# Which early tile takes its second layer direct, and where batch 1's Fourier units stand, in a kernel of spectral mixing and a two-layer network

## The chip, the cores and the metric

The kernel runs on one core of a Trainium2 chip. TensorE (PE) multiplies matrices into PSUM, VectorE (DVE) and ScalarE (ACT) read PSUM and write SBUF, GpSimd (POOL) works on SBUF alone, and SyncE (SP) only issues transfers; GpSimd's queue issues transfers too. Each engine takes its instructions in the order of the program. The metric is the device time of one execution in microseconds (us), as a median of several runs.

## The reference

The input x has 8 batches of 3008 rows and 256 channels. Each batch goes through a real Fourier transform along the rows, is multiplied by a filter of 1505 frequencies, and goes back; then all 24064 rows pass a network of 256, 2048 and 256 channels with an exact Gelu.

```python
X = np.fft.rfft(x, axis=1)
Y = X * (filt_r + 1j * filt_i)[None, :, :]
y = np.fft.irfft(Y, n=x.shape[1], axis=1)      # 8 x 3008 x 256
h = y.reshape(24064, 256) @ w_in               # 256 -> 2048
g = 0.5 * h * (1.0 + erf(h / np.sqrt(2.0)))
out = g @ w_out                                # 2048 -> 256
```

## The kernel before

**Tiles and slots.** The network works on 47 tiles of 512 rows. A tile has 16 slots; slot s of the program is slot s mod 16 of tile s // 16. In each slot `mm1` (L640) makes one sixteenth of the tile's first layer, two matmuls of 512 columns, and ScalarE turns it into g by a Gelu (L643). Between them stands a sixteenth of the second layer of the tile before. Everything else is put into the slots by hand, with a table `at` that maps slots to calls; calls of a slot are emitted ahead of its matmuls.

**Second layer.** Most tiles use `mm2_seven` (L714): seven products of half-size matrices in place of eight, 112 matmuls of 128 columns, 7 a slot. They need sums of quarters of g, which VectorE makes on SBUF in the tile's last slots and the next tile's first ones: `sums_1` (L685, four instructions), `sums_2` (L691, two) and `sums_3` (L696, two, into s4_sb), and small adds of PSUM results (L729 to L743). A tile in the list `plain` uses `mm2_first` (L656) in their place: 64 matmuls of 256 columns, 4 a slot, no sums, two copies (L660). Before the change `plain` is tiles 0 and 2. The last tile of batch 0, tile 5, has another pace (`late`): in its first six slots stands only the second layer of tile 4.

**Fourier work.** Batch 0 is transformed in the prologue, up to about 38 us. Batches 1 to 7 are transformed beside the network. For a batch: `load_x_pairs` (GpSimd's queue) brings x, `fold` (VectorE, L109, L110) adds and subtracts its halves, `s1` is stage 1 (L430), whose results go through DRAM (R1) and come back as b_sb with `r1` (SP's queue). Three units follow, each with `s2` (stage 2, L457), `s2_out` (four products with the filters Fu on VectorE, L468), `s2_sum` (four sums, L474 and L475), `s3` (stage 3, L488) and its evacuation `s3_out` into v_sb, from where it goes through DRAM (R2) and returns as d_sb with `r2`. `s4` (stage 4, L515) multiplies d_sb with the table T4a and writes the rows y that `mm1` reads. The slots of batch 1's units are `s2 = (30, 44, 58)`, with stage 3 eleven slots later; `r2` of its first quarter comes four slots behind the last stage 3, and the first `s4` stands at slot 82, which does not depend on these.

**Filters and tables.** The filters are loaded into F, and `move_filters` copies them from SBUF to SBUF into Fu on SP's queue, by quarters c = 0 to 3: 16 moves in the prologue for a unit's first pair, 20 at slot 18 for the other two units. When F is read out its memory is used anew: s4_sb, v_sb and T4a all lie in it. T4a is made by `table_4_all` on GpSimd in four parts of six instructions (L410, L412), before the change at slots 47, 54, 101 and 114, from the factors that `table_4_factors` makes at slot 38. Scratch tiles tmp_sb for it and the d_sb tiles share a pool of three buffers.

**Gates.** `gate` (L142) is a GpSimd copy of one element. It makes GpSimd's queue wait until that element has been written, and with it all that stands behind: `load_next` puts one ahead of each group of x loads. For the last groups of batch 2 it reads d_sb of batch 1. One gate at slot 101 reads the last a_sb of batch 2's stage 1.

**Output rows.** `put_rows` (L761) issues them, mostly on GpSimd's queue, for tiles 0 and 1 partly on SP's. The buffers (ost and t_sb) are four, used in turn.

**PSUM.** Three banks are of kind h (first layer, one of stage 2 and one of stage 3), two of kind o (second layer), three of kind f (the other banks of stages 1 to 3, and table factors).

Of the kernel before, what the change touches and what calls it, by code (L numbers as in the profile page):

```python
# [31 lines left out]
class _Mix:  # L32
# [87 lines left out]

    def move_filters(self, m0, m):

        for c in range(4):
            for q in range(2):
                for e in range(2):
                    o, k = 32 * c + 16 * q, 6 * c + m0
                    for t in ((0, 1),) if c or m0 == 0 else ((0,), (1,)):
                        t = slice(t[0], t[-1] + 1)
                        i = self.F[32 * q + e:32 * q + 32:2, t, k:k + m, :]
                        self.nc.sync.dma_start(  # L130
                            out=self.Fu[o:o + 16, t, e ^ q, m0:m0 + m, :].rearrange("p t m c -> p t (m c)"),
                            in_=i.rearrange("p t m c -> p t (m c)"))
# [281 lines left out]
    def s1(self, b, c):  # L414

        nc = self.nc
        if c == 0:
            self.st[b, "R1"] = self.dram.tile([NB, 48, 256], BF16, tag="R1", name="R1")
        if b == 1 and c == 3:
            at = self.pp.tile([128, 2, 4, 256], BF16, tag="p12", name="p12").rearrange("p t k c -> p (t k) c")  # L420
        else:
            at = self.pa.tile([128, 8, 256], BF16, tag="a", name="a_sb")
        self.st[b, "a"] = at
        x = self.st[b, "s", c], self.st["x1"][:, 1, 4 * c:4 * c + 4]
        lent = "o" if b == 1 and c < 2 else "h"
        ps = [[self.bank("ps_s1", lent if i == v == 0 else "f") for v in range(2)] for i in range(2)]
        for i in range(2):
            for d in range(2):
                for v in range(2):
                    nc.tensor.matmul(ps[i][v][64 * d:64 * d + 64, :], lhsT=self.T1s[64 * v:64 * v + NA],  # L430
                                     rhs=x[d][64 * v:64 * v + NA, 2 * i:2 * i + 2, :], start=True, stop=True)
        for i in range(2):
            for v in range(2):
                w = 4 * v + 2 * i
                self._evac(at[:, w:w + 2, :].rearrange("p w c -> p (w c)"), ps[i][v], "act" if v else False)
        for d in range(2):
            for v in range(2):
                w = HB * d + 16 * v + 4 * c
                nc.sync.dma_start(out=self.st[b, "R1"].rearrange("n q c -> q n c")[:, w:w + 4],
                                  in_=at[64 * d:64 * d + 48, 4 * v:4 * v + 4])  # L440
# [204 lines left out]
    def mm2_first(self, t, lo, hi):  # L645

        nc = self.nc
        for n in range(lo, hi):
            if t:
                q, jc = n // 16, n % 16  # L650
            else:
                jc, q = (n // 2, n % 2) if n < 32 else (n % 16, n // 16)
            if jc == 0 and (q % 2 == 0 if t else q < 2):
                self.st["o2", q // 2 if t else q] = self.bank("ps_o", "o").rearrange("p (a b) -> p a b", a=2)
            ps, a = (self.st["o2", q // 2], q % 2) if t else (self.st["o2", q % 2], q // 2)
            nc.tensor.matmul(ps[:, a, :], lhsT=self.st["g", t][:, jc, q * 128:q * 128 + 128],  # L656
                             rhs=self.w_out_sb[:, jc, :], start=(jc == 0), stop=(jc == 15))
            if jc == 15 and (q % 2 if t else q > 1):
                ost = self.po.tile([128, 2, 256], FP32, tag="ost", name="ost")
                nc.vector.tensor_copy(out=ost, in_=ps)  # L660
                for i in range(2):
                    self.put_rows(t * TCH + ((q - 1 + i) if t else (q - 2 + 2 * i)) * 128, ost[:, i],
                                  nc.gpsimd if t else nc.sync)

    def weight_sums(self):

# [116 lines left out]
def kernel(  # L783
# [9 lines left out]
    m = _Mix(ctx, tc, x, filt_r, filt_i, moe_w_in, moe_w_out, out)  # L793
    nc, B, S = tc.nc, m.B, m.S
# [3 lines left out]
    g = m.small  # L798
# [109 lines left out]
    at = {}  # L908

    def put(slot, f, *a):  # L910
        at.setdefault(slot, []).append((f, a))

    def first(b):
        return (b * S // TCH) * 16

    busy, crowd, after = set(), set(), {}
    for b in range(1, B):
        hi = first(b)
        e = 4 * (b == B - 1)
        s1, n1, r1 = (4, 3.3, 17) if b == 1 else (hi - 87, 3.7, hi - 73) if b == 2 else (hi - 94 - e, 3.7, hi - 80 - e)  # L920
        s2 = (30, 44, 58) if b == 1 else (hi - 74, hi - 59, hi - 44) if e else (hi - 64 + (b == 2), hi - 48, hi - 32)
        busy.update(range(s1 - 1, s1 + int(3 * n1) + 2))
        for c in range(4):
            slot = (4, 8, 11, 13)[c] if b == 1 else s1 + int(c * n1)
            put((0, 1, 5, 8)[c] if b == 1 else (70, 74, 86, 94)[c] if b == 2 else hi - 94 - (20, 13, 8, 6)[c], m.fold, b, c)
            put(slot, m.s1, b, c)
        for u in range(3):
            put(r1 if u < 2 else s2[0] + 1, m.r1, b, u)
            put(s2[u], m.s2, b, u)
            for i in range(4):  # L930
                put(s2[u] + 2 * i + (b == 2 and u == 0), m.s2_out, b, u, i // 2, i % 2)
            for i in range(2):
                put(s2[u] + (9 + i if 1 < b < B - 1 else 7 + 2 * i), m.s2_sum, b, 2 * u + i)
            s3 = s2[u] + (11 if b == 1 else 12 if e or (b, u) in ((2, 0), (B - 2, 2)) else 13)
            put(s3, m.s3, b, u)
            put(s3 + 1, m.s3_out, b, u, 1)
            busy.update(range(s2[u] - 1, s2[u] + 5), range(s3 - 1, s3 + 2))
        after[b] = s3 + 4
        crowd.update(range(s2[0], after[b]), range(s1 + 66, s1 + 94))
        if b + 1 < B:  # L940
            for i, (u, o, p) in enumerate(((0, 5, 1), (0, 7, 1), (1, 1, 2), (1, 5, 3), (1, 7, 3), (2, 1, 4), (2, 5, 5), (2, 7, 5))):
                put((76, 77, 80, 81)[i - 4] if b == 1 and i > 3 else s2[u] + o, m.load_next, b, p, i // 2, i % 2)
# [27 lines left out]
    put(9, m.table_u_pick, g)  # L970
    put(9, m.table_4_rows, g)
    put(9, m.weights_4, g)
    put(24, m.table_u)
    put(38, m.table_4_factors, g)
    put(101, lambda: m.gate(m.st[2, "a"][0:1, 3, 0:1]))
    parts = [(w, h) for w in range(0, HB, 8) for h in range(2)]
    for i, slot in enumerate((47, 54, 101, 114)):
        put(slot, m.table_4_all, parts[2 * i:2 * i + 2])
    put(18, m.move_filters, 2, 4)
    put(20, m.weight_sums)  # L980
    plain = (0, 2)
    seven = [t for t in range(NT) if t not in plain]
    for t in seven:
        for i, s in enumerate((12, 13, 15, 16 if t == S // TCH - 1 else 17)):
# [6 lines left out]
    for s in range((NT + 1) * 16):  # L991
        t, jc = s // 16, s % 16
# [44 lines left out]
```

## Time and profile before

| | |
|---|---|
| median of 3 runs | 738.75 us (738.12 to 739.8) |
| profiled execution | 738.78 us, its span 736.7 us |
| VectorE's products L468 | 84 x 1217 ns |
| VectorE's sums L685, L691, L696 | 180 x 690, 90 x 687, 90 x 697 ns |
| output rows on GpSimd's queue L761 | 231 x 575 ns |
| x loads on GpSimd's queue L101 | 156 x 516 ns |
| moves of filters at slot 18 | 20, issued from 55.94 to 69.9 us |
| first Gelu of tiles 1, 2, 3, 4, 6 | 52.87, 65.10, 81.39, 96.59, 130.50 us |

A row of a timeline has the start in us from the span's start, the duration in us, the engine, the line of the kernel, the operation, the tile written and those read with their shapes, and how many such instructions were put together (x2). In brackets stands for how long the engine had been idle before it, and on whom it waited. Matmul ends are modelled, so what is exact of a matmul is its start. Where several instructions are put together, their pitch is the distance to the next start divided by their number.

### The profile page before, as it was taken

To read this page: it belongs to the slowest core of one execution; us is meant where nothing else is said; L and a number is where in the kernel's file an instruction comes from. 1 tells how busy PE (TensorE), PEld (TensorE's weight loads), DVE (VectorE), ACT (ScalarE), POOL (GpSimd) and SP (SyncE) were. 2 spreads that over 40 slices of the span, in tenths; PEclk is the share of its full clock that TensorE was granted. 3 is DMA by queue.
4 is the path that set the end of the run, shared out by engine and by line. 5 is a ranking of instruction groups with operands and counts; after the bars stand their busy time and mean duration, and the time that the engine had idled before them with its cause. 6 is when DMAs were issued, how large, how long until landed. Compare 5 with 4: busy or idle time off the path is not lost.

```text
span 736.7 us, 22328 instructions
## 1 busy us (share of the span) xinstructions
PE 723.3 (98%) x9213; PEld 506.1 (69%) x9213; DVE 602.8 (82%) x1105; ACT 575.6 (78%) x1049; POOL 285.9 (39%) x545
## 2 busy tenths in 40 slices
PE   8999999999999999999999999999999999999998
PEld 4755665677777766676677767666677767777776
DVE  8886797899887998789986989779998898675566
ACT  6997766788887888778887788877888788777773
POOL 7943745686122653134521355114631131122121
PEclk9999999999999999999999999999999999999999
DMA  9885526655345553555545455455544433311011
GB/s 147 155 183 135 150 77 131 190 155 107 86 126 177 123 101 101 146 149 119 115 126 172 104 113 125 116 151 132 121 108 126 149 101 108 103 39 49 30 58 59
DMA packets 81254, 87.73 MB, mean 119 GB/s; under 512 B 13393, under 2 KB 61137, under 8 KB 81153
## 3 DMA queue, kind: packets, MB, share of 16 engines
q0 software_dynamic: 22288, 39.50, 24.1%
q1 hardware_dynamic: 58449, 46.62, 23.2%
q8 instruction: 72, 1.18, 0.7%
q10 hardware_dynamic: 416, 0.20, 0.1%
q14 instruction: 29, 0.24, 0.1%
HBM read 54.00 MB, written 46.66 MB: 137 GB/s over the span
## 4 chain that ended last, share of the span: by engine, by line
PE 87%; POOL 4%; DMA 3%; issue 3%; DVE 3%; ACT 1%; SPq 0%; DVEq 0%; POOLq 0%
PE ps_h L640 40%; PE ps_o L714 36%; PE ps_s L515 3%; PE ps_s L430 2%; PE ps_s L488 1%; DMA b_sb<-R 1%; PE ps_s L457 1%; POOL tmp_sb L410 1%; POOL out_dram L761 1%; DMA x_sb<-in_x_dram 1%; PE ps_c L587 1%; ACT y_sb L325 1%; POOL x_sb L101 1%; PE ps_o L656 1%; PE ps_c L565 0%
## 5 line engine op out<-in xcount | busy, mean ns | idle before, releaser
L643 ACT ACTIVATE g_sb<-ps_h 128x512 f16<-128x512 f32 x752 | 445.5, 602 | 137.2 <-PE ps_h L640 129.0
L640 PE MATMUL ps_h<-y_sb,w_in_sb 128*128 128x512 bf16 (+3 forms) x1600 | 445.4, 366 | 1.5 <-DVE a_sb L327 1.2
L761 POOL DMA_DIRECT2D out_dram<-ost x231 | 131.4, 575 | 373.9 <-DVE ost L743 365.5
L714 PEld LDWEIGHTS <-g_sb 128*128 128x128 f16 x2880 | 188.8, 98 | 83.4 <-issue 14.6
L640 PEld LDWEIGHTS <-w_in_sb 128*128 128x128 bf16 x1600 | 125.7, 98 | 9.3 <-issue 2.9
L714 PE MATMUL ps_o<-w_sums,g_sb 128*128 128x128 f16 x1440 | 124.8, 219 | 0.4 <-DVE g_sb L691 0.2
L714 PE MATMUL ps_o<-w_sums,s_sb 128*128 128x128 f16 x1440 | 123.3, 219 | 0.0
L714 PEld LDWEIGHTS <-s_sb 128*128 128x128 f16 x1440 | 97.0, 98 | 37.5 <-issue 2.1
L685 DVE TENSOR_TENSOR s_sb<-g_sb 128x1024 f16<-128x1024 f16 x180 | 118.6, 690 | 0.7 <-ACT g_sb L643 0.6
L714 PE MATMUL ps_o<-w_out_sb,g_sb 128*128 128x128 f16 x1440 | 116.4, 219 | 0.1
L468 DVE TENSOR_TENSOR p<-ps_s,Fu 128x1024 bf16<-128x1024 f32 x84 | 101.9, 1217 | 8.9 <-PE ps_s L457 7.3
L101 POOL DMA_DIRECT2D x_sb<-in_x_dram x156 | 79.5, 516 | 1.9 <-DMA x_sb<-in_x_dram 0.7
L691 DVE TENSOR_TENSOR g_sb<-s_sb,g_sb 128x1024 f16<-128x1024 f16 x90 | 61.7, 687 | 1.5
L696 DVE TENSOR_TENSOR F<-g_sb 128x1024 f16<-128x1024 f16 x90 | 62.8, 697 | 0.0
L714 PE MATMUL ps_o<-w_out_sb,F 128*128 128x128 f16 x720 | 62.5, 219 | 0.0
L714 PEld LDWEIGHTS <-F 128*128 128x128 f16 x720 | 48.3, 98 | 16.0 <-issue 0.8
L736 DVE TENSOR_TENSOR t_sb<-t_sb,ps_o 128x256 f32<-128x256 f32 x45 | 18.8, 417 | 41.9 <-PE ps_o L714 41.4
L515 PEld LDWEIGHTS <-d_sb 96*128 96x128 bf16 x448 | 31.3, 97 | 26.1 <-issue 1.3
L325 ACT ACTIVATE F<-ps_s 128x512 bf16<-128x512 f32 x83 | 45.5, 608 | 3.3 <-PE ps_s L488 3.2
L325 ACT ACTIVATE y_sb<-ps_s 128x376 bf16<-128x376 f32 x95 | 45.5, 479 | 3.2 <-PE ps_s L515 3.2
L743 DVE TENSOR_TENSOR ost<-t_sb,ps_o 128x256 f32<-128x256 f32 x88 | 32.9, 415 | 14.0 <-PE ps_o L714 14.0
L327 DVE CAST a_sb<-ps_s 128x512 bf16<-128x512 f32 x54 | 34.7, 684 | 11.3 <-PE ps_s L430 11.1
(159 smaller groups left out, 574.6 us busy)
## 6 DMA issues: line engine op xcount, KB each, us to landing
out_dram<-ost POOLq DMA_DIRECT2D x127, 128.0 KB, 2.9
b_sb<-R SPq DMA_DIRECT2D x21, 512.0 KB, 4.9
R<-F SPq DMA_DIRECT2D x84, 128.0 KB, 2.4
d_sb<-R SPq DMA_DIRECT2D x56, 192.0 KB, 3.8
R<-a_sb SPq DMA_DIRECT2D x108, 96.0 KB, 2.2
x_sb<-in_x_dram POOLq DMA_DIRECT2D x48, 94.0 KB, 2.6
x_sb<-in_x_dram POOLq DMA_DIRECT2D x48, 48.0 KB, 2.7
x_sb<-in_x_dram POOLq DMA_DIRECT2D x12, 188.0 KB, 5.1
```

The costliest lines, as they stand in the source:

```text
L101: self.nc.gpsimd.dma_start(out=xt[64 * v + to:64 * v + to + m, h, 4 * c:4 * c + 4 * n, :], in_=xv[h][at:at + m, w:w + 4 * n, :])
L325: self.nc.scalar.activation(out=out, in_=in_, func=AF.Copy, scale=1.0 if scale is None else scale)
L327: self.nc.vector.tensor_copy(out=out, in_=in_)
L468: v(out=w[:, a], in0=ps.unsqueeze(2).to_broadcast([128, 2, 2, 256]), in1=f.unsqueeze(1).to_broadcast([128, 2, 2, 256]), op=ALU.mult)
L515: nc.tensor.matmul(ps[:, 94 * i:94 * i + 94], lhsT=d[:, (grp % 2) * 4 + i, 128 * half:128 * half + 128], rhs=self.T4a[:, 4 * grp + i, 0:2 ...
L640: nc.tensor.matmul(ps[:, o:o + n], lhsT=w[:, dc], rhs=self.ring[:, dc, off:off + n], start=(dc == 0), stop=(dc == 1))
L643: nc.scalar.activation(out=self.st["g", t][:, jc, :], in_=ps, func=AF.Gelu)
L685: self.nc.vector.tensor_tensor(out=self.st["s", t][:, i:i + 2], in0=a, in1=b, op=ALU.subtract)
L691: self.nc.vector.tensor_tensor(out=a21[:, k], in0=self.st["s", t][:, k, 0], in1=a22[:, k], op=ALU.add)
L696: self.nc.vector.tensor_tensor(out=self.s4_sb[:, k], in0=a12[:, k], in1=s2[:, k], op=ALU.subtract)
L714: nc.tensor.matmul(ps[:, (m + 1) % 2, sub, :], lhsT=a[:, i, 128 * sub:128 * sub + 128], rhs=b[:, i], start=i == 0, stop=i == 7)
L761: eng.dma_start(out=out, in_=tile_[lo - r0:lo - r0 + n])
```

## The change

Tile 1 becomes the direct one, and tile 2 takes the seven products. Batch 1's stage 2 moves from slots 30, 44, 58 to 26, 39, 53, with stage 3 at 37, 51, 65 (before 41, 55, 69); with them `r2`'s first quarter (73 to 69) and the first four x loads of batch 2 (35, 37, 45, 49 to 31, 33, 40, 44). The four table parts move to slots 67, 82, 98 and 105, and ahead of the first three stands a gate on the last sum of tile 3, 4 or 5; the gate on a_sb goes. The table factors move from 38 to 48, `table_u` from 24 to 23. The quarters of `move_filters` are taken in reversed order. Since the two-copy form now has tile 1, its last row block goes to SP's queue, as in the seven-product form.

```diff
     def move_filters(self, m0, m):
-        for c in range(4):
+        for c in (3, 2, 1, 0):
...
             at = self.pa.tile([128, 8, 256], BF16, tag="a", name="a_sb")
-        self.st[b, "a"] = at
...
-                                  nc.gpsimd if t else nc.sync)
+                                  nc.gpsimd if t > 1 or t and q + i < 4 else nc.sync)
...
-        s2 = (30, 44, 58) if b == 1 else (hi - 74, hi - 59, hi - 44) if e else (hi - 64 + (b == 2), hi - 48, hi - 32)
+        s2 = (26, 39, 53) if b == 1 else (hi - 74, hi - 59, hi - 44) if e else (hi - 64 + (b == 2), hi - 48, hi - 32)
...
-            s3 = s2[u] + (11 if b == 1 else 12 if e or (b, u) in ((2, 0), (B - 2, 2)) else 13)
+            s3 = s2[u] + ((11, 12, 12)[u] if b == 1 else 12 if e or (b, u) in ((2, 0), (B - 2, 2)) else 13)
...
-    put(24, m.table_u)
-    put(38, m.table_4_factors, g)
-    put(101, lambda: m.gate(m.st[2, "a"][0:1, 3, 0:1]))
+    put(23, m.table_u)
+    put(48, m.table_4_factors, g)
+    for t, slot in ((3, 67), (4, 82), (5, 98)):
+        put(slot, lambda t=t: m.gate(m.st["s", t][0:1, 7, 1, 255:256]))
     parts = [(w, h) for w in range(0, HB, 8) for h in range(2)]
-    for i, slot in enumerate((47, 54, 101, 114)):
+    for i, slot in enumerate((67, 82, 98, 105)):
         put(slot, m.table_4_all, parts[2 * i:2 * i + 2])
...
-    plain = (0, 2)
+    plain = (0, 1)
```

## The prediction

> **What bounds the kernel now.** I read the page first, then the waits, then the timelines of the stretch from 55 to 135 us, engine by engine.
>
> ```profile
> PE 723.3 (98%) x9213; PEld 506.1 (69%) x9213; DVE 602.8 (82%) x1105; ACT 575.6 (78%) x1049; POOL 285.9 (39%) x545
> PEclk9999999999999999999999999999999999999999
> ```
>
> TensorE is busy for 98% of the span at a granted clock of 0.999, and the change takes no matmul away. So only time in which TensorE stands can be won. A late tile without any Fourier work takes 13.16 us (first Gelu of tiles 45 and 46: 701.29 and 714.45), which is 16 slots of 0.82. Tiles 2 to 5 took 65.40 us (first Gelu of tile 2 at 65.10, of tile 6 at 130.50). Their work, priced at pitches of undisturbed stretches: 4 x 13.16, plus 0.8 for the direct tile, 5 stage-2 and stage-3 blocks x 0.6, 4 stage-4 blocks x 0.166, 3 stage-1 blocks x 0.67 and 0.5 for the table factors = 59.6. So about 5.8 us are lost there, and from tile 6 on next to nothing. TensorE's timeline shows where:
>
> ```profile
> 71.99 0.42 PE L488 MATMUL ps_s<-p,U 32*64 32x256 bf16 x16
> 73.25 0.65 PE L488 MATMUL ps_s<-p,U 32*64 32x256 bf16 x16 [0.84 <-DVE p L474]
> ...
> 99.99 0.42 PE L488 MATMUL ps_s<-p,U 32*64 32x256 bf16 x16
> 101.94 0.65 PE L488 MATMUL ps_s<-p,U 32*64 32x256 bf16 x16 [1.52 <-DVE p L474]
> ...
> 121.49 0.28 PE L714 MATMUL ps_o<-w_out_sb,F 128*128 128x128 f16 x2
> 123.01 1.02 PE L640 MATMUL ps_h<-y_sb,w_in_sb 128*128 128x512 bf16 x4 [1.25 <-DVE a_sb L327]
> ```
>
> Stage 3 of units 0 and 2 of batch 1 stands between its halves, because VectorE's stage-2 sums (L474) are late: 73.25 against 72.28 and 101.94 against 100.27 (a half takes 0.28), 0.97 + 1.67 us. At 121.5 the next matmul is 1.41 late for an evacuation. With 0.37 at 113.9 that is 4.4 us in four places; the rest up to 5.8 is small change around them. I take 5.5 as what can be won, nearer to the sum over the tiles because that also has the small change; 4.4 and 5.8 are its ends.
>
> Why VectorE is late: in slots 28 to 41 it does tile 1's sums (L685, L691, L696) and unit 0's products together, and later GpSimd's table parts stretch it:
>
> ```profile
> 58.96 1.28 DVE L685 TENSOR_TENSOR s_sb<-g_sb 128x1024 f16<-128x1024 f16 x2
> ...
> 71.06 0.42 DVE L475 TENSOR_TENSOR p<-p 128x512 bf16<-128x512 bf16 x1
> ...
> 84.66 1.20 DVE L474 TENSOR_TENSOR p<-p 128x512 bf16<-128x512 bf16 x1
> ...
> 92.54 2.06 DVE L685 TENSOR_TENSOR s_sb<-g_sb 128x1024 f16<-128x1024 f16 x2
> ```
>
> (The same kinds take 0.42 and 1.28 undisturbed, 1.20 and 2.06 beside GpSimd's L410 and L412.)
>
> The stop at 121.5 is the end of another chain, read in GpSimd's and VectorE's rows:
>
> ```profile
> 112.23 0.18 POOL L142 COPY gate<-d_sb 1x1 bf16<-1x1 bf16 x1 [12.38 <-DMA d_sb<-R]
> 116.26 2.89 POOL L761 DMA_DIRECT2D out_dram<-ost  x5
> ```
>
> ```profile
> 119.67 0.42 DVE L737 TENSOR_TENSOR ost<-t_sb,ps_o 128x256 f32<-128x256 f32 x1 [1.71 <-DMA out_dram<-ost]
> 120.34 0.68 DVE L109 TENSOR_TENSOR x_sb<-x_sb 111x1024 bf16<-111x1024 bf16 x1
> ```
>
> GpSimd's queue stands 12.38 us at the gate for batch 1's first stage-4 tile; behind it are batch 2's x loads and tile 3's output rows; a buffer of these holds L737, and fold and evacuation stand behind L737.
>
> **The change part by part.**
>
> *Direct tile.* Tile 1's second layer (64 matmuls of 256 columns, a slot 0.87) runs beside tile 2, and tile 2's seven products beside tile 3. The 0.8 us moves a tile ahead: net 0. VectorE is relieved in slots 28 to 40 of 4 x 0.69 + 2 x 0.69 + 2 x 0.70 = 5.5 us of sums and has them in 44 to 56 instead; the seven small adds (0.42 each) go the same way and two copies (0.69 each) the other. This decides units 0 and 2 below.
>
> *Unit 0 at slot 26.* TensorE reaches it at 59.2; b_sb of unit 0 landed at 58.73 in the trace's record of its semaphore. Its four products (pitch 1.13) and four sums (pitch 0.34), with the copy of tile 0, end at about 66.2; stage 3 at slot 37 comes at 68.6. The 0.97 and its restart go. Stage 3's evacuation writes where the moved filters lie (v_sb is a part of F): with the reversed order quarter 1 is moves 9 to 12, issued by 64.8, quarter 2 moves 5 to 8; at the median of 2.6 both have landed by about 67.4, and the evacuation comes after 69.
>
> *Unit 1 at slot 39.* TensorE is there at 70.9, the first product at 71.6 if all 20 moves of the second filter set have landed. In the profile the last was issued at 69.32 and landed near 71.6. But batch 2's first x loads now start near 63, not 69.93, under these moves. Bounds: 0 and 2.5 us later (the worst landing of these moves, 5.1, against the median 2.6). VectorE's work until stage 3 at slot 51 (8 products and sums, two copies, tile 2's sums) ends near 81, TensorE is there at 83: 2 us of cover hide all but 0.5 of the upper end, so I take 0, ends 0 and 0.5.
>
> *Two slots between stage 3 and the next stage 2* (37 to 39, 51 to 53; before 41 to 44, 55 to 58). Stage 2 needs three banks of kind f that stage 3 fills. In the profile ScalarE frees them 2.0 and 2.6 us after stage 3's end at 73.9 (75.37 1.10 for the last two). Two slots and half a stage 2 are 2.0 us: 0.5 lost the first time, 0.2 the second, where VectorE takes one of the four. Ends 0 and 1.3. New cost 0.7.
>
> *Unit 2 at slot 53.* From the product at 85.6 VectorE has 4 products, 4 sums, two L696, two L685 and five small adds until stage 3 of slot 65: 4 x 1.13 + 4 x 0.34 + 4 x 0.61 + 1.9 = 10.2 us. TensorE needs 12 x 0.82 + 0.6 = 10.4. Before it was 11 slots with 1.3 us of stretching (0.8 + 0.56), and 1.67 were lost. I take 0.3 lost, ends 0 and 1.9.
>
> *Table parts.* Parts 1 and 2 (5.6 us each: 79.91 to 85.58; 6.2 under load, 90.13 to 96.34) leave slots 47 to 58, where they stretched VectorE by some 2.9 us (four L474 and L475 from 82.97 take 3.2 for 1.7, the pair at 92.54 0.8 more, an L685 at 95.65 0.56 more). Part 1 now waits for tile 3's last sum (slot 65), then runs from about 100.5 to 106.5 beside tile 4's folds and sums. VectorE's work in that tile is 13 instructions of 0.6 and 8 of 0.35, 10.6 of 13.2 us, so 2.6 are to spare; stretching seven instructions by 0.4 is 2.8. I take 0, ends 0 and 0.7. Three gates more on GpSimd: 0.2 each, in idle time. Behind the new gate in GpSimd's queue stand the x loads and tile 3's output rows.
>
> [...]
>
> *Gate and chain.* Stage 3 of unit 2 is four slots earlier. From its end (102.6) to the gate's release (112.23) is 9.6 us; from 96.7 this gives 106.3, about when table part 1 ends (106.5). Then 4.0 us to the rows (112.23 to 116.26) and 3.4 to L737's release (116.26 to 119.67): 114.1. TensorE's side of L737 was ready at 118.0; with 3.3 us won by then, 114.7. The 1.41 and the 0.37 go, with 0.6 us in hand; I keep 0.3, ends 0 and 1.4.
>
> *Third stage-4 transfer.* Its d_sb now lies in the buffer of table part 3, so the SP queue waits at slot 108 for it and stage 2's last load of batch 2 stands behind. Part 3 ends near 134.5 and slot 108 is near 136; the data is needed at slot 121, 10.7 us later, and such a transfer takes 3.8: covered by 6 us, 0. Without that cover each us of part 3's lateness would be one of TensorE's.
>
> *Moves in the prologue.* All 16 now wait for the last filter loads (quarter 3 first), so they start near 22 and not at 13.46, and end near 34; SP's next work is at 43.65: 0. GpSimd's copy at 18.90 waits for a filter load beside which they ran; ends -1.5 (VectorE's wait of 1.56 at 19.97 gone) and 0. I take -0.1, since these moves were some 5% of the DMA share there.
>
> *One row of tile 1 to SP, table_u and table factors moved:* behind VectorE's copy, 0.
>
> Sum: -5.5 + 0.7 + 0.3 + 0.3 - 0.1 = -4.3. The profiled execution took 738.78 us (span 736.7 and 2.1 around it), 0.03 from the median of 738.75: 734.45, so 734.5 us. All upper ends of the costs together (0.5 + 1.3 + 1.9 + 0.7 + 1.4, on 4.4 won) are +1.4, all lower ends -7.3.
>
> **Rivals.** *VectorE stays late (A).* It now has tile 2's sums and units 1 and 2 in 26 slots, saturated again; for it 10.2 against 10.4 us. Each 1 us there is 1 us for TensorE and for the chain behind. Loss 1.0 to 2.3: 735.5 to 736.8.
>
> *GpSimd becomes the bound (B).* Gate, part 1, x loads and rows make an unbroken chain of 0.2 + 6 + 4 + 3.4 us from tile 2's rows on. If it is 2 to 4 us late (VectorE's late sums, output issues of 0.59), L737 and the fold wait again: 736.8 to 738.5. Against it: it has 12.38 us less standing.
>
> *Slower (C).* Parts 3 and 4 run back to back in tile 6, from 128 to 140, where VectorE was busy 7.7 and 9.2 of 10 us and idle 3.1 of 20. Twelve GpSimd instructions (8 x 0.82 + 4 x 1.0), each holding up an evacuation of stage 1 or a sum as long as it lasts, are up to 10.5 us. It decides from 3.1 + 4.3 = 7.4 us on, and at 10.5 gives 738.75 - 4.3 + 7.4 = 741.9: 739 to 742. Against it: six of them ran at 135.35 to 141 without a stop of TensorE.
>
> *More won (D):* all 5.8, the prologue's 1.5 and no new loss: 731.5 to 732.9.
>
> **How the numbers follow.** Forecast (732.9 to 735.5) 0.55, A 0.18, B 0.11, C 0.11, D 0.05. The range 732.6 to 737.0 holds the forecast, A, and a little of B and D: somewhat under 0.8. A difference of 0.2% (1.5 us) is about what a measurement can tell from no change. Faster (below 737.3): 0.55 + 0.18 + 0.05 and 0.03 of B = 0.81. Same: 0.08 of B and 0.02 of C = 0.10. Slower: the rest of C, 0.09.
>
> **What would show it.** Stage 3 of unit 0 and 2 without [<-DVE p L474]; first product of unit 1 without a wait for a DMA; no stop before L640 at stage 1 of batch 2; table parts outside tile 3 and no gate of 12 us; tile 6's first Gelu near 126. Wrong, if a stop of over 1 us stands at slot 65, if L737 waits for out_dram, or if tiles 6 and 7 grow.

## The result and the profile after

The changed kernel takes 736.7 us (median of 10 runs) where the kernel before takes 738.98 in the same comparison: a ratio of 0.9968, 95% interval 0.9957 to 0.998, or 2.4 us (1.5 to 3.2) faster. The forecast was 734.5. The direction was right, and so were the places where time was to be won; a little over half of the gain came.

TensorE is as full as before, at a mean granted clock of 1.000 (before 0.999). From the changed kernel's page, busy time and the granted clock by slices:

```profile
PE 724.0 (99%) x9213; PEld 506.4 (69%) x9213; DVE 604.5 (82%) x1105; ACT 575.4 (78%) x1049; POOL 287.6 (39%) x547
PEclk9999999999999999999999999999999999999999
```

VectorE is busy 1.7 us longer than before (602.8) for the same 1105 instructions: something lengthens them. The profiled execution took 736.53 us, its span 734.4. In the code of the changed kernel all lines beyond 423 are one lower than before (the Gelu is L642, stage 3 L487, the sums L684, L690, L695, the stage-2 sums L473 and L474).

I compare two points: the first Gelu of tile 2 (65.10 before, 64.46 after) and that of tile 8 (160.52, 158.33). The way between them is 95.41 us before and 93.87 after; I call it the early stretch. It leaves out the prologue, whose end differs by over 2 us among the fourteen profiles of this study (first Gelu between 37.9 and 40.3). So 0.64 of the profiled 2.25 us are won ahead of the stretch, 1.54 in it, and the rest of the program takes the same (within 0.1). Expected in the stretch were 4.2.

TensorE's timeline of the changed kernel, the same places as before and three new ones:

```profile
67.76 0.64 PE L487 MATMUL ps_s<-p,U 32*64 32x256 bf16 x32
...
95.30 0.64 PE L487 MATMUL ps_s<-p,U 32*64 32x256 bf16 x32
...
110.30 0.84 PE L713 MATMUL ps_o<-w_out_sb,g_sb 128*128 128x128 f16 x12 [1.02 <-DVE ost L742]
...
119.86 1.02 PE L639 MATMUL ps_h<-y_sb,w_in_sb 128*128 128x512 bf16 x4 [0.35 <-DVE a_sb L327]
...
145.92 0.59 PE L639 MATMUL ps_h<-y_sb,w_in_sb 128*128 128x512 bf16 x2 [0.80 <-DVE p L467]
```

Stage 3 of units 0 and 2 now stands as one row of 32 matmuls: the stops of 0.84 and 1.52 are gone. The stop in front of L639 (1.25, then the end of the gate's chain) is down to 0.35. But at 109 and 145 stand new ones, each behind a VectorE instruction that comes late. VectorE's timeline shows why:

```profile
99.33 1.31 DVE L109 TENSOR_TENSOR xs<-x_sb 111x1024 bf16<-111x1024 bf16 x1
100.67 2.13 DVE L110 TENSOR_TENSOR x_sb<-x_sb 111x1024 bf16<-111x1024 bf16 x1
...
104.12 1.30 DVE L109 TENSOR_TENSOR x_sb<-x_sb 111x1024 bf16<-111x1024 bf16 x1
105.46 1.20 DVE L110 TENSOR_TENSOR x_sb<-x_sb 111x1024 bf16<-111x1024 bf16 x1
106.58 0.41 DVE L735 TENSOR_TENSOR t_sb<-t_sb,ps_o 128x256 f32<-128x256 f32 x1
...
109.50 0.74 DVE L742 TENSOR_TENSOR ost<-t_sb,ps_o 128x256 f32<-128x256 f32 x2
...
142.54 1.47 DVE L684 TENSOR_TENSOR s_sb<-g_sb 128x1024 f16<-128x1024 f16 x1
```

and GpSimd's what ran beside the first four:

```profile
100.65 1.60 POOL L410 TENSOR_TENSOR tmp_sb<-t_sb 96x376 f32<-96x376 f32 x2
102.33 1.32 POOL L412 TENSOR_TENSOR F<-tmp_sb 96x376 bf16<-96x376 f32 x1
103.73 2.38 POOL L410 TENSOR_TENSOR tmp_sb<-t_sb 96x376 f32<-96x376 f32 x2
106.19 1.32 POOL L412 TENSOR_TENSOR F<-tmp_sb 96x376 bf16<-96x376 f32 x1
```

The folds L109 and L110 take 0.69 elsewhere; here they take 5.94 for 2.76. L735 and L742, which read PSUM, do not lengthen (0.41, and 0.74 for two, where L742 takes 0.75 for two at 126.68 with no table part beside it), but stand behind the folds, and TensorE waits at 109 for L742. Between the first fold and L742 VectorE is never idle for more than 0.04 us. At 142.54 it is parts 3 and 4 of the table (130.56 to 143.46) and a sum L684.

### The profile page after: what moved, and what is told of

It is laid out like the page before. It is cut to its first block, busy times and chain, and to the rows that moved or that the text cites. A ratio compares the mean times of both kernels' runs of the same rounds, so it can differ in the third digit from the quotient of the medians.

```text
span 734.4 us, 22333 instructions
## 1 busy us (share of the span) xinstructions
PE 724.0 (99%) x9213; PEld 506.4 (69%) x9213; DVE 604.5 (82%) x1105; ACT 575.4 (78%) x1049; POOL 287.6 (39%) x547
## 3 DMA queue, kind: packets, MB, share of 16 engines
q8 instruction: 72, 1.18, 0.7%
## 4 chain that ended last, share of the span: by engine, by line
PE 85%; DVE 5%; DMA 4%; POOL 1%; issue 1%; ACT 1%; SPq 1%; DVEq 0%; POOLq 0%; ACTq 0%
PE ps_h L639 40%; PE ps_o L713 37%; PE ps_s L514 3%; PE ps_s L429 2%; PE ps_s L487 1%; PE ps_s L456 1%; DMA x_sb<-in_x_dram 1%; DVE s_sb L684 1%; PE ps_o L655 1%; DMA w_out_sb<-in_moe_w_out_dram 1%; DMA b_sb<-R 1%; SPq L130 1%; POOL F L137 1%; DMA F<-in_filt_i_dram 1%; ACT b_sb L325 1%
## 5 line engine op out<-in xcount | busy, mean ns | idle before, releaser
L642 ACT ACTIVATE g_sb<-ps_h 128x512 f16<-128x512 f32 x752 | 445.7, 601 | 138.4 <-PE ps_h L639 130.0
L639 PE MATMUL ps_h<-y_sb,w_in_sb 128*128 128x512 bf16 (+3 forms) x1600 | 445.5, 366 | 1.5 <-DVE p L467 0.8
L713 PEld LDWEIGHTS <-g_sb 128*128 128x128 f16 x2880 | 188.7, 98 | 84.2 <-issue 15.0
L639 PEld LDWEIGHTS <-w_in_sb 128*128 128x128 bf16 x1600 | 125.8, 98 | 9.3 <-issue 3.0
L713 PE MATMUL ps_o<-w_sums,g_sb 128*128 128x128 f16 x1440 | 124.7, 219 | 0.3 <-DVE g_sb L690 0.2
L713 PE MATMUL ps_o<-w_sums,s_sb 128*128 128x128 f16 x1440 | 123.3, 219 | 0.0
L713 PEld LDWEIGHTS <-s_sb 128*128 128x128 f16 x1440 | 97.1, 98 | 37.6 <-issue 2.1
L684 DVE TENSOR_TENSOR s_sb<-g_sb 128x1024 f16<-128x1024 f16 x180 | 119.8, 697 | 0.4 <-ACT g_sb L642 0.3
L713 PE MATMUL ps_o<-w_out_sb,g_sb 128*128 128x128 f16 x1440 | 116.5, 219 | 1.0 <-DVE ost L742 1.0
L467 DVE TENSOR_TENSOR p<-ps_s,Fu 128x1024 bf16<-128x1024 f32 x84 | 101.9, 1218 | 12.3 <-PE ps_s L456 10.7
L690 DVE TENSOR_TENSOR g_sb<-s_sb,g_sb 128x1024 f16<-128x1024 f16 x90 | 61.8, 688 | 1.5
L713 PE MATMUL ps_o<-w_out_sb,F 128*128 128x128 f16 x720 | 62.5, 219 | 0.0
L695 DVE TENSOR_TENSOR F<-g_sb 128x1024 f16<-128x1024 f16 x90 | 61.5, 683 | 0.0
L713 PEld LDWEIGHTS <-F 128*128 128x128 f16 x720 | 48.3, 98 | 16.0 <-issue 0.8
L735 DVE TENSOR_TENSOR t_sb<-t_sb,ps_o 128x256 f32<-128x256 f32 x45 | 18.8, 418 | 39.7 <-PE ps_o L713 39.2
L742 DVE TENSOR_TENSOR ost<-t_sb,ps_o 128x256 f32<-128x256 f32 x88 | 32.9, 416 | 13.6 <-PE ps_o L713 13.6
L327 DVE CAST a_sb<-ps_s 128x512 bf16<-128x512 f32 x54 | 34.7, 684 | 11.3 <-PE ps_s L429 11.1
```

Of the source, the lines that this page charges most:

```text
L327: self.nc.vector.tensor_copy(out=out, in_=in_)
L467: v(out=w[:, a], in0=ps.unsqueeze(2).to_broadcast([128, 2, 2, 256]), in1=f.unsqueeze(1).to_broadcast([128, 2, 2, 256]), op=ALU.mult)
L639: nc.tensor.matmul(ps[:, o:o + n], lhsT=w[:, dc], rhs=self.ring[:, dc, off:off + n], start=(dc == 0), stop=(dc == 1))
L642: nc.scalar.activation(out=self.st["g", t][:, jc, :], in_=ps, func=AF.Gelu)
L684: self.nc.vector.tensor_tensor(out=self.st["s", t][:, i:i + 2], in0=a, in1=b, op=ALU.subtract)
L690: self.nc.vector.tensor_tensor(out=a21[:, k], in0=self.st["s", t][:, k, 0], in1=a22[:, k], op=ALU.add)
```

## The experiments

My theory (T1) is that GpSimd's table parts lengthen those VectorE instructions beside them that have two inputs in SBUF, and that this is the missing 2.5 us. The rivals: VectorE's own load in tiles 4 and 6 is too high whatever GpSimd does (R1), or GpSimd's chain of gates is late (R2). For the time won ahead of the stretch: the reversed order of the moves (P1), or scatter between executions (P2).

All ratios are to the kernel before on the same chip; the early stretch is from one profile each.

| kernel | ratio and 95% interval | early stretch, us |
|---|---|---|
| before | 1 | 95.41 |
| changed kernel | 0.9968 (0.9957 to 0.998) | 93.87 |
| changed, tables cut to nothing | 0.9934 (0.9922 to 0.9946) | 91.37 |
| before, tables cut to nothing | 0.9986 (0.9975 to 0.9996) | 94.01 |
| changed, old order of moves | 0.9974 (0.9964 to 0.9984) | 94.26 |
| changed, old direct tile | 0.9975 (0.9964 to 0.9985) | 94.66 |
| changed, old table layout | 1.0002 (0.9988 to 1.0017) | 98.00 |
| changed, old slots of units | 1.0082 (1.0068 to 1.0095) | 101.26 |
| before, new direct tile only | 1.0074 (1.0057 to 1.0092) | 101.63 |
| before, new table layout only | 1.0074 (1.0057 to 1.0091) | 100.21 |
| changed, table instructions halved | 0.9971 (0.9958 to 0.9985) | 94.34 |
| changed, parts 1 and 2 early | 0.995 (0.9937 to 0.9963) | 93.04 |
| changed, part 1 early | 0.9959 (0.9942 to 0.9977) | 91.87 |
| changed, part 1 early, part 2 after a fold | 0.9944 (0.9931 to 0.9956) | 91.44 |

### Tables cut to nothing, in both kernels

```diff
-                tt(out=o, in0=self.fcs[:, w:w + 8, h, x:x + 1].to_broadcast([96, 8, NA]),
-                   in1=self.G[:, x].unsqueeze(1).to_broadcast([96, 8, NA]), op=ALU.mult)
-            tt(out=to[:, h, w:w + 8], in0=a, in1=b, op=ALU.add)
+                tt(out=o[:, 0:1, 0:2], in0=self.fcs[:, w:w + 1, h, x:x + 1].to_broadcast([96, 1, 2]),
+                   in1=self.G[:, x, 0:2].unsqueeze(1).to_broadcast([96, 1, 2]), op=ALU.mult)
+            tt(out=to[:, h, w:w + 1, 0:2], in0=a[:, 0:1, 0:2], in1=b[:, 0:1, 0:2], op=ALU.add)
```

> The changed kernel with each of GpSimd's 24 table instructions cut to one or two elements; gates, queue order, buffers and slots stay. The table arithmetic is left out, so stage 4 computes with a wrong table; no other work changes. T1 (the table parts lengthen VectorE's folds and sums beside them, and that is the missing part of the gain): the three stops at 109.1, 119.2 and 144.8 us go (1.02, 0.35 and 0.80), folds L109 and L110 take 0.69 everywhere, and the time falls by 2.0 to 2.5 us against the changed kernel (736.7 to about 734.4). R1 (VectorE's own load in tiles 4 and 6 is too high): the stop for ost L742 at 109 and the one for p L467 at 145 stay, gain below 0.5 us. R2 (GpSimd's chain of gates): the stops move with the gates' releases; the parts being 5.6 us shorter each, gain 0.5 to 1.0.

> The kernel before with the same cut of the 24 table instructions (table arithmetic left out, all else as it was). T1: the parts cost the old kernel too, in slots 47 to 58, where VectorE was stretched by some 2.9 us: the stop of 1.52 at 101.9 and the one of 1.25 at 123.0 shrink, gain 1.5 to 2.5 us (738.98 to about 737). If T1 gains as much here as in the changed kernel, the change has only moved that cost. R1: gain below 0.5 in both.

Nearly all of the table's arithmetic is left out of these two kernels, so stage 4 works with a wrong table; nothing else is changed. Measured: 734.13 us for the changed kernel so cut, 737.7 for the kernel before. In the early stretch the tables cost 93.87 - 91.37 = 2.50 us after the change, and 95.41 - 94.01 = 1.40 before it; the ratios say 2.5 and 1.0. The second is less than the 1.5 to 2.5 that were expected: in the kernel before, the stop of 1.52 before stage 3 of unit 2 falls to 0.47, but the one behind the gate stays at 1.18. In the changed kernel all three stops are gone. VectorE's timeline of the changed kernel with cut tables, the same four folds:

```profile
100.00 0.68 DVE L109 TENSOR_TENSOR xs<-x_sb 111x1024 bf16<-111x1024 bf16 x1
100.72 0.69 DVE L110 TENSOR_TENSOR x_sb<-x_sb 111x1024 bf16<-111x1024 bf16 x1
...
102.72 0.68 DVE L109 TENSOR_TENSOR x_sb<-x_sb 111x1024 bf16<-111x1024 bf16 x1
103.44 0.69 DVE L110 TENSOR_TENSOR x_sb<-x_sb 111x1024 bf16<-111x1024 bf16 x1
```

VectorE's own instructions are the same in this run, so R1 falls. The gates and the order of the queues are the same too, but the parts are shorter, and so GpSimd's chain is earlier; against R2 stand the changed kernel's own rows, where VectorE runs on with no gap above 0.04 us up to L742 and so waits there for no gate and no transfer. The first L109, begun at 99.33, ends just where the record of the first L410 begins (100.65). That it too is held up by the table shows with the cut tables, where it takes 0.68, and with the halved ones below, where it takes 1.00. T1 also says how much the change is worth without tables in both: 94.01 - 91.37 = 2.64 in the stretch, of which 1.1 was handed back to dearer tables.

### Halved table instructions: a wait for the whole instruction, or a share by time?

```diff
-            for o, x in ((a, 0), (b, 1)):
-                tt(out=o, in0=self.fcs[:, w:w + 8, h, x:x + 1].to_broadcast([96, 8, NA]),
...
+            for k in (0, 4):
+                for o, x in ((a, 0), (b, 1)):
+                    tt(out=o[:, k:k + 4], in0=self.fcs[:, w + k:w + k + 4, h, x:x + 1].to_broadcast([96, 4, NA]),
...
```

> The changed kernel with each table instruction split in two of half the width: 48 in place of 24, the same arithmetic. From the cut-down run, an instruction of almost no width takes 0.17 us, so a half takes about 0.49 in place of 0.80 and a part some 6.9 us in place of 5.6. If VectorE waits for the end of the one GpSimd instruction that is running (a lock per instruction), its longest delay falls from 0.78 to about 0.47 and VectorE's whole lengthening from 6.3 to 4 or 4.5 us; the stops shrink, 0.5 to 1.2 us won (735.4 to 736.1). If the two engines share bandwidth, the lengthening goes by the time they overlap: 6.3 us or more, and the time stays or grows by up to 0.5 us.

VectorE's timeline of this kernel (one line of code more, so its numbers are those of the kernel before):

```profile
98.73 1.00 DVE L109 TENSOR_TENSOR xs<-x_sb 111x1024 bf16<-111x1024 bf16 x1
99.76 1.49 DVE L110 TENSOR_TENSOR x_sb<-x_sb 111x1024 bf16<-111x1024 bf16 x1
...
102.63 0.99 DVE L109 TENSOR_TENSOR x_sb<-x_sb 111x1024 bf16<-111x1024 bf16 x1
103.65 0.95 DVE L110 TENSOR_TENSOR x_sb<-x_sb 111x1024 bf16<-111x1024 bf16 x1
```

Halving the GpSimd instruction halves what one fold loses: 0.31 in place of 0.62 (both L109), 0.80 in place of 1.44 (the first L110). That fits a wait for the end of the running GpSimd instruction, and not a loss that goes by the time the two overlap; what holds VectorE up in it no row shows. Added up over VectorE's rows beside the tables the loss fell only from 6.3 to 5.3 us, where 4 to 4.5 was expected, because part 1 now takes 9.2 us (99.74 to 108.9) in place of 6.9, and reaches more sums. The stop for ost shrank from 1.02 to 0.52, the one for L467 at 145 stayed (0.78). But behind part 1 stand gate, x loads and output rows, all later now, and so what rival B foresaw appears, further down in the same timeline:

```profile
115.82 0.42 DVE L737 TENSOR_TENSOR ost<-t_sb,ps_o 128x256 f32<-128x256 f32 x1 [1.23 <-DMA out_dram<-ost]
```

The stop for a_sb behind it grew from 0.35 to 1.05, and the time did not move. What one fold loses fell about as expected; the gain did not come.

### One part of the change undone, or done alone

The direct tile back in the changed kernel (`plain = (0, 2)`), and alone in the kernel before (`plain = (0, 1)`):

> The changed kernel with tile 2 direct again in place of tile 1 (and the row block back on GpSimd's queue). The prediction's step: VectorE has 5.5 us of tile 1's sums back in slots 28 to 40, beside unit 0 at slot 26, and its stage-2 sums come late: a stop of 1 to 2.5 us before stage 3 at slot 37, time +1 to +2 us (737.7 to 738.7 where the changed kernel takes 736.7). Rival: only the table layout and the slots matter, VectorE's load there does not: within 0.4 us of the changed kernel.

> The kernel before with only the direct tile moved (tile 1 in place of 2, and its last row block to SP). By the prediction's steps: the stop of 0.97 us before stage 3 of unit 0 goes with VectorE's relief in slots 28 to 41, while that of unit 2 (1.67) and the one behind the gate (1.41) stay: 0.7 to 1.0 us won, 738.0 to 738.3. The rival (VectorE's load has only moved): tile 2's sums now stand in slots 44 to 56 beside unit 1's products and both early table parts, stage 3 of unit 1 at slot 55 or unit 2's stop grows by 1 to 2 us: no gain or a loss, 738.8 to 740.

Undone, it costs 0.8 us in the stretch where 1 to 2 were expected, and 0.5 by the ratios, which their intervals do not tell from nothing. But its stop is the one that the prediction's step names, before stage 3 of unit 0. TensorE's timeline:

```profile
67.56 0.42 PE L487 MATMUL ps_s<-p,U 32*64 32x256 bf16 x16
69.47 0.65 PE L487 MATMUL ps_s<-p,U 32*64 32x256 bf16 x16 [1.49 <-DVE p L473]
```

Alone it loses 5.5 us, far beyond what either theory had. By the rows, the old slots put unit 1's stage-2 sums, tile 2's sums and table parts 1 and 2 (79.57 to 86.2, 88.85 to 95.1) into the same 15 us of VectorE. TensorE's timeline of the kernel before with the direct tile moved:

```profile
86.75 0.51 PE L714 MATMUL ps_o<-w_sums,g_sb 128*128 128x128 f16 x6 [1.78 <-DVE g_sb L691]
...
91.06 0.32 PE L488 MATMUL ps_s<-p,U 32*64 32x256 bf16 x8 [0.65 <-DVE p L474]
92.17 0.44 PE L488 MATMUL ps_s<-p,U 32*64 32x256 bf16 x8 [0.80 <-DVE p L475]
92.55 0.93 PE L714 MATMUL ps_o<-w_sums,s_sb 128*128 128x128 f16 x7
```

The last line is worth a look: seven matmuls that take 0.55 take 0.93. More on this below.

The table layout back in the changed kernel, and alone in the kernel before:

```diff
+        self.st[b, "a"] = at
...
-    put(48, m.table_4_factors, g)
-    for t, slot in ((3, 67), (4, 82), (5, 98)):
-        put(slot, lambda t=t: m.gate(m.st["s", t][0:1, 7, 1, 255:256]))
+    put(38, m.table_4_factors, g)
+    put(101, lambda: m.gate(m.st[2, "a"][0:1, 3, 0:1]))
...
-    for i, slot in enumerate((67, 82, 98, 105)):
+    for i, slot in enumerate((47, 54, 101, 114)):
```

(The first expectation speaks of a run that is told of further down.)

> The changed kernel with the table's old layout: factors at slot 38, parts at 47, 54, 101 and 114, the gate on a_sb at 101, no gates on tile sums. T1 (parts cost where VectorE's instructions with two SBUF inputs are dense): the stops at 109.1, 119.2 and 144.8 go (2.5 us won), but parts 1 and 2 now run beside tile 2's sums and unit 1's stage-2 sums, where the run with the parts at slot 36 had a stop of 1.4 us for ost L659 at 81.5; I expect 1.5 to 2.5 us lost there, so between -1.0 and 0 us against the changed kernel (735.6 to 736.6). If the three stops stay without parts beside them, T1 is wrong. The new table layout is then worth between 0 and -1 us within the change, not the 1.8 us that the gate's 1.41 and 0.37 were booked at.

> The kernel before with only the new table layout (factors 48, gates on tile sums, parts 67, 82, 98, 105). By what the cut-down tables showed: the old layout costs the kernel before 1.4 us between slots 32 and 116, the new one cost the changed kernel 2.5 us there. T1: parts 1 to 4 meet the same folds and sums of tiles 4 to 6, so +1.1 us (740.1 where the kernel before takes 739.0), with stops near 112 and 148 like those at 109.1 and 144.8 of the changed kernel, and the stop for p L474 at 101.9 shrunk from 1.52 to 0.5. The prediction's own view (table parts cost nothing, gate and stretch go): -1.5 to -2. On the prologue: it has the old order of moves, and P1 (the order moves the prologue) has its first Gelu of slot 10 within 0.6 us of the kernel before, later than in all kernels with the reversed order.

Both expectations missed on size. With the old layout the three stops do vanish, but the one beside tile 2's sums is 3.35 us, not 1.5 to 2.5. TensorE's timeline of that kernel, with the line numbers of the kernel before:

```profile
89.06 0.63 PE L457 MATMUL ps_s<-b_sb,T2p 64*32 64x256 bf16 x16 [3.35 <-DVE F L327]
```

So the new layout is worth 4.1 us of the stretch inside the change in this profile, and 2.5 us by the ratios. Alone in the kernel before it loses 5.5 us: there the stop before stage 3 of unit 2 did not shrink to 0.5 but became two, of 1.70 and 0.80.

The slots of the units back in the changed kernel, `s2 = (30, 44, 58)` and stage 3 eleven slots later:

> The changed kernel with batch 1's units back at slots 30, 44, 58 and stage 3 eleven slots later. With the table parts gone from slots 47 to 58, the 6 us that the direct tile alone lost there do not come back. The prediction's steps: unit 2 has eleven slots, a stop of 0.5 to 1 us before its stage 3; its last stage is four slots later, so the gate's release and part 1 move from 100 to 107 us later by up to 3 us and with them the stop for ost L742: +1 to +2 us (737.7 to 738.7). Rival: the slots are worth nothing by themselves, and spare the 0.7 us of the narrow gaps for bank f: within 0.5 of the changed kernel or 0.5 better.

This expectation was off most: some 8 us slower than the changed kernel for a forecast of 1 to 2. The place was right. TensorE, VectorE and GpSimd in the timelines of this kernel:

```profile
99.16 0.42 PE L487 MATMUL ps_s<-p,U 32*64 32x256 bf16 x16
102.33 0.32 PE L487 MATMUL ps_s<-p,U 32*64 32x256 bf16 x8 [2.74 <-DVE p L473]
103.45 0.44 PE L487 MATMUL ps_s<-p,U 32*64 32x256 bf16 x8 [0.81 <-DVE p L474]
103.82 0.93 PE L713 MATMUL ps_o<-w_sums,g_sb 128*128 128x128 f16 x7
```

```profile
98.97 0.68 DVE L684 TENSOR_TENSOR s_sb<-g_sb 128x1024 f16<-128x1024 f16 x1
...
100.62 1.65 DVE L473 TENSOR_TENSOR p<-p 128x512 bf16<-128x512 bf16 x1
102.20 1.20 DVE L474 TENSOR_TENSOR p<-p 128x512 bf16<-128x512 bf16 x1
```

```profile
100.39 1.60 POOL L410 TENSOR_TENSOR tmp_sb<-t_sb 96x376 f32<-96x376 f32 x2
```

Part 1 stands behind the gate on tile 3's last sum, L684 at 98.97; here GpSimd's queue comes to the gate only at 100.09, behind six output rows. In the changed kernel unit 2's stage-2 sums are done by then (the last ended at 95.29). With the old slots two of them come after that sum, at 100.62, just when part 1 begins: 2.85 us in place of 0.83, with stage 3 waiting. That is the same in the kernel before with the new layout alone (L474 at 100.04 took 1.65, L475 at 101.61 1.19). Later the gate on d_sb opens at 114.28 in place of 107.44 (up to 3 us later was expected), and TensorE waits 2.05 us for a_sb at 127.77. So the new layout needs the new slots: the gate shields the stage-2 sums only if the unit stands early enough. The new slots alone were not run.

The order of moves back in the changed kernel (`for c in range(4)`):

> The changed kernel with the quarters of the moves in the old order 0 to 3. P1 (the reversed order frees the prologue, because the moves wait for the last filter load and leave the queues to the loads): the first Gelu comes 0.7 to 1.1 us later again, time +0.7 us. P2 (the prologue's 0.7 to 1.1 us is scatter of the transfers between executions): first Gelu within 0.3 us, time within 0.3. If units 1 or 2 of batch 1 need the reversed order, a stop stands at the first product of unit 1 or at stage 3 of unit 0, by up to 1 us.

736.97 us, within the intervals the same as the changed kernel. No stop appears at unit 0 or 1, but the early stretch is 0.4 longer. The first Gelu over all profiles: nine kernels with the reversed order have 37.91 to 39.49, mean 38.66; five with the old one 39.11 to 40.31, mean 39.72. The two groups overlap, and by the first Gelu of tile 2 the difference is 0.8 (means 64.49 and 65.27). This speaks for P1, by 0.8 to 1 us on the mean; a single pair of profiles shows nothing, and the timed comparison, 0.4 us with some 1.1 to either side, neither confirms nor excludes it. The rows show the step that P1 names: the moves are issued from 21.31 on in the changed kernel, from 13.46 in the kernel before and from 13.66 with the order back, and VectorE's longest wait in its prologue products is 0.62, 1.56 and 1.21.

### Other places for the table parts

```diff
-    put(48, m.table_4_factors, g)
-    for t, slot in ((3, 67), (4, 82), (5, 98)):
-        put(slot, lambda t=t: m.gate(m.st["s", t][0:1, 7, 1, 255:256]))
+    put(34, m.table_4_factors, g)
+    put(98, lambda: m.gate(m.st["s", 5][0:1, 7, 1, 255:256]))
...
-    for i, slot in enumerate((67, 82, 98, 105)):
+    for i, slot in enumerate((36, 36, 98, 114)):
```

> The changed kernel with the table parts laid out anew: factors at slot 34, parts 1 and 2 at slot 36 with no gate (VectorE stands idle there from 65.8 to 70.9 us), part 3 at slot 98 behind its gate, part 4 at slot 114. T1: no part lies beside the folds of tiles 4 and 5 nor two of them beside tile 6's sums, so the stops at 109.1 and 119.2 go and that at 144.8 shrinks; stretching returns in slots 36 to 48 beside unit 0's and 1's products with two idle stretches to take it: gain 1.0 to 2.5 us against the changed kernel (734.2 to 735.7). R1: no gain, or a loss of up to 1 us from later products of unit 1. R2: x loads of batch 2 (slots 40 and 44) wait behind 12 us of table work on GpSimd's queue, a stop at stage 1 of batch 2 of up to 2 us, no gain.

735.55 us, at the edge of what was expected, and by the intervals not quite to be told from the changed kernel. The stops at 109, 119 and 145 are gone; but T4a lies in the memory of F, so the first L412 waited 3.62 us for the moves out of it, the parts ran mostly from 71.75 to 81.8 and not in VectorE's idle time, and lengthened the sums ahead of a copy L659: a stop of 1.38 at 83.06. VectorE's timeline shows which instructions lengthen and which do not; beside all four rows GpSimd makes the table:

```profile
71.73 1.23 DVE L467 TENSOR_TENSOR p<-ps_s,Fu 128x1024 bf16<-128x1024 f32 x1 [5.87 <-ACT F L325]
72.87 0.68 DVE L659 COPY ost<-ps_o 128x512 f32<-128x512 f32 x1
73.47 2.35 DVE L467 TENSOR_TENSOR p<-ps_s,Fu 128x1024 bf16<-128x1024 f32 x2
75.73 1.07 DVE L684 TENSOR_TENSOR s_sb<-g_sb 128x1024 f16<-128x1024 f16 x1
```

So only part 1 was left there, with part 2 at slot 82 behind the gate on tile 4:

> The changed kernel with factors at slot 34, part 1 at 36 without a gate, part 2 at 82 behind the gate on tile 4's sum, part 3 at 98 behind that on tile 5's, part 4 at 114. T1: part 1 runs from about 71.7 (when the moves out of F have landed) to 77, mostly beside products L467, which do not lengthen; the stop at 81.5 of the run with both parts early goes or falls below 0.4, those at 109.1 and 144.8 stay gone, the one at 119.2 stays at most 0.35: 2.0 to 2.4 us won against the changed kernel, 734.2 to 734.6, the best of all with a full table. R1: no better than the run with both parts early (735.55).

The early stretch came out as expected, 91.87. The time did not: 736.22, with runs from 734.16 to 739.63, which is not to be told from the kernel with both parts early, nor from the changed kernel. Its profile has one wait of 0.50 us for d_sb at 460, which the changed kernel does not have; the cut tables had one of 0.73 at the same place. Whether it is there in most runs is open.

At 118.9 this kernel still waits 0.42 us for a_sb, behind folds (1.03 and 1.19) beside part 2. The last kernel moves part 2 behind the fold:

```diff
-    for t, slot in ((4, 82), (5, 98)):
-        put(slot, lambda t=t: m.gate(m.st["s", t][0:1, 7, 1, 255:256]))
+    put(87, lambda: m.gate(m.st["x1"][0:1, 1, 11, 255:256]))
+    put(98, lambda: m.gate(m.st["s", 5][0:1, 7, 1, 255:256]))
...
-    for i, slot in enumerate((36, 82, 98, 114)):
+    for i, slot in enumerate((36, 87, 98, 114)):
```

> The changed kernel with factors at 34, part 1 at slot 36, part 2 at slot 87 behind a gate on the fold of slot 86, part 3 at 98 behind its gate, part 4 at 114. T1: as the run with one part early, but part 2 begins after the folds at 115 and 116.4, so these take 0.69 and the stop of 0.42 for a_sb L327 at 118.9 goes or halves: 0.2 to 0.4 us better than that run between slots 32 and 116 (-3.7 to -3.9 against the kernel before), in time 0.9945 to 0.996 of the kernel before. If a wait for d_sb at 460 us shows again, 0.5 of it is given back there.

734.39 us, a ratio of 0.9944 (0.9931 to 0.9956): the fastest with a whole table, and faster than the changed kernel by their intervals, which just do not overlap. Its early stretch, 91.44, is that of the kernel without tables (91.37). TensorE's timeline at the three places of the stops:

```profile
107.92 1.73 PE L713 MATMUL ps_o<-w_out_sb,g_sb 128*128 128x128 f16 x28
...
117.94 1.05 PE L639 MATMUL ps_h<-y_sb,w_in_sb 128*128 128x512 bf16 x4
...
143.62 0.55 PE L713 MATMUL ps_o<-w_sums,g_sb 128*128 128x128 f16 x7
```

GpSimd does the same 24 instructions; what changed is that beside them VectorE mostly runs products and copies that read PSUM. What VectorE loses beside them falls from 6.3 to 1.8 us, and TensorE waits for none of that.

## Why the prediction was right and where it was not

The measured 736.7 lies inside the stated range of 732.6 to 737.0, but not where the forecast stood (732.9 to 735.5): it lies where the range had made room for rival A, and A is not what happened. Units 1 and 2 did not stop TensorE. So that the range held is in part luck. Of the signs named, those of the gain came (stage 3 in one piece, no gate of 12 us), and one of being wrong came too: tiles 6 and 7 grew, from 30.02 to 30.98 us. Step by step:

- **Direct tile, units 0, 1 and 2.** Right. Stage 3 of units 0 and 2 has no stop. Unit 1's first product (70.88) waits for TensorE and for no move. The direct tile is what keeps unit 0 free (1.49 back when undone). Unit 2 was booked at 0.3 lost and lost nothing.
- **Two slots between stage 3 and the next stage 2.** Booked at 0.7; TensorE loses 0.49 at 70.55 and 0.28 at 84.70 between two stage-2 matmuls, behind an evacuation of ScalarE: 0.77. The mechanism and the size were right.
- **Gate and chain.** Right in substance: L736 of tile 5 (115.74) no longer waits for output rows. The 0.35 that is left comes from the table: the fold L110 at 117.13, beside part 2, takes 1.47, and with cut tables the stop is gone. The gate on d_sb opened at 107.44 where 106.3 was booked, and with a part 1 longer by 2.3 us (halved instructions) the wait for output rows was back; so there was little in hand.
- **Third stage-4 transfer, one row to SP, table factors.** No wait shows.
- **Moves in the prologue.** Booked at -0.1 between -1.5 and 0. The profiled pair has -1.08 at the first Gelu and -0.64 at tile 2; the means over the profiles say -0.8. Too small, inside its ends.
- **Table parts.** This step failed. It was booked at 0, with 0.7 as its end, and measured 2.50. The stretching in tile 4 came out about as booked in all, 3.18 us against 2.8, though as four folds of 0.51 to 1.44 and not as seven instructions of 0.4. The error was in the cover: 2.6 us to spare in tile 4 were set against it, as if VectorE's idle time of a tile could be spent anywhere in it. The folds stand ahead of L735 to L742 in VectorE's order, TensorE needs L742 at a fixed point, and the idle time of the tile lies elsewhere. The same step looked at part 1 alone; parts 3 and 4, back to back beside tile 6's sums, cost 0.96 more between the first Gelu of tile 6 and that of tile 8. That is rival C at a fraction of its price: its evacuations read PSUM and did not lengthen (two L327 at 130.80 took 1.28 and the L329 at 137.48 and 140.05 0.54 each, as with no part beside them), its sums lost 1.84 us. Nor did the step put a price in TensorE's time on what the old layout had cost: 1.40 by the cut tables.
- **Which instructions lengthen.** The step took 0.4 for each of seven. In the rows it goes by where the inputs lie: products L467, with one input in PSUM, take 1.21 to 1.23 beside the tables (parts 1 and 2 early), 1.22 elsewhere; a fold or sum with both inputs in SBUF loses up to 0.78 in the changed kernel (the L110 at 117.13, beside an L410 of 0.81), once 1.44 (the first L110), and about half as much when the GpSimd instruction is halved (0.31 for 0.62 at L109). To part 1 TensorE lost 1.02, at L742; the 2.50 are of all four parts.

The sum with what was measured: without tables the early stretch is 95.41 - 91.37 = 4.04 shorter than before, against 4.2 booked. With the 0.77 for the gaps that is 4.81 won where 5.5 was taken, between its ends of 4.4 and 5.8; this is a remainder and not a sum of stops. Then -4.81 + 0.77 + 2.50 = -1.54 in the stretch, -0.64 before it and -0.07 behind it: the profiled -2.25. The miss of 2 us is the one term of 2.50, softened by the prologue, where 0.64 came for 0.1 booked. All these are differences of single profiles.

## What to carry to other kernels

Idle time of an engine over a tile is no cover: what counts is the idle time between the lengthened instruction and the next one that TensorE waits for. Put GpSimd's arithmetic beside VectorE instructions that read PSUM (L467 took 1.21 to 1.23 there, 1.22 elsewhere), or behind a gate on the last two-input instruction of the group; here that alone was worth 2.4 us of the early stretch. And where a change moves three things at once, undo them one at a time before pricing them apart: the direct tile alone or the table layout alone lost 5.5 us against the kernel before, the set without its slots 6, while the set without the direct tile lost only some 0.5 of its gain.

## What the runs showed of the hardware beyond that

**A long stop can be paid for twice.** In the profiles of the four kernels that ended slowest, with a stop of over 2.5 us or several close together, TensorE's granted clock then fell to a half. The changed kernel with the old slots, by windows (window, its length, TensorE busy with its instructions, granted clock, DMA share, GB/s):

```profile
96.00:99.30 3.30, 2.97 (x40) 1.00 0.24 80
99.30:103.50 4.20, 0.65 (x32) 0.88 0.19 63
103.50:105.00 1.50, 1.50 (x16) 0.50 0.00 0
...
109.00:112.00 3.00, 3.00 (x34) 0.94 0.21 48
```

In finer windows the clock was at a half from about 102.5 to 109.4 here, from 87.9 to 94.7 in the kernel with the old table layout, and for 3.4 us (92.2 to 95.6, 103.4 to 106.8) in the two where one part was done alone. Seven matmuls L713 that take 0.55 then take 0.93. By estimate, from the clock of 0.50, that costs up to half of such a stretch, 1.7 or 3.4 us, and is part of why all four were slower than expected. In the profiles of the kernels before and after, with stops of up to 1.52 us, the clock was 1.00 throughout the early stretch. Not in every run, though: of the 66 runs of the kernel before that stand beside the experiments, 22 show a mean clock of 0.998 or less and 44 one of 0.999 or more, and the 22 are about 1 us longer in the median (739.9 against 738.7); the ten runs of the changed kernel all show 1.00. Where the clock fell in those runs is not shown. In the 3.4 us before it fell, TensorE had been busy for 0.67 in the changed kernel with the old slots, and for 1.24 with the old table layout; what makes it fall no run shows.

**A tiny GpSimd instruction is cheap.** With two elements a partition in place of 376, six of the eight pairs of L410 took 0.34 us, and the two beside VectorE's folds and sums of tile 4 0.81 and 0.89, against 1.60 for the whole pair at 100.65 in the changed kernel.
